# The product of V for the last 64 positions, before instead of behind the fourth product of V, in two of four batches

## The chip, the cores and the metric

The program runs on one core of a Trainium2 chip. Its time is the device time of one execution in microseconds (us). The engines are TensorE (PE; its weight loads are PEld), VectorE (DVE), ScalarE (ACT), GpSimd (POOL) and SyncE (SP), which issues the DMAs. Every engine has its own instruction queue, and engines wait for one another at semaphores.

## The reference

Three blocks follow one another, all in float32, over 4 batches of 576 positions and 512 features:

```
attention   8 heads of 64, window of 128 positions, a bias by distance; out = softmax(q k^T) v
gMLP        h = gelu(x @ w_in)              # 512 -> 1024
            u, v = h[:, :512], h[:, 512:]
            v_n = normalize(v) * g_ln       # mean and variance over the 512 features
            v_s = w_sg @ v_n + b_sg         # over the 576 positions
            x   = x + (u * v_s) @ w_out
GLU         h = relu(x @ w_in2); c = conv of 3 taps along the positions
            out = (h * sigmoid(c)) @ w_out2
```

The change concerns the products that make v in the gMLP of the first and of the last batch.

## The kernel before, in words

The kernel keeps about float32 accuracy with three matmuls where one would do in a single pass: each matrix is split into a high and a low part (tiles `hi`, `lo`), and hi*hi, hi*lo and lo*hi are added up in PSUM.

The work is cut into steps, and a written list gives their order. Letters name the kind of step, numbers the batch and the part. Lower-case steps prepare data, many of them weights: they clamp and rebuild numbers out of 64-bit words with five DVE instructions for each piece (lines 310 to 315, tile `wa`), and split them on ACT and POOL. The steps of the gMLP are:

- `V b.j` (function `m_v`): v for 128 positions (j = 0 to 3), 12 matmuls of 512 columns into a PSUM tile `psv`. j = 4 is the rest of 64 positions: four copies on POOL put the high and low parts of the last 64 positions side by side into tiles `xt`; then 8 matmuls run, and the two halves of the PSUM tile are added: ACT copies one half out (line 755), DVE adds the other (line 756, in the trace DVE L231 `v<-psv,v`). Only that addition frees the PSUM tile. With j < 4 one ACT instruction, the gelu, reads the tile and frees it.
- After that each V step goes through gelu, mean and variance (DVE L760, L761), the inverse root on POOL (L763, L764), the normalization (DVE L765) and the split into `vn` (ACT L222 the high part, DVE L231 the low part).
- `U b.half.m` (`m_u`): u, 12 matmuls into a PSUM tile `psu`, and a gelu on ACT.
- `G b.half.m` (`m_sg`): the product with w_sg, 14 matmuls into `pss`. It reads all five `vn` tiles of its batch, the one of j = 4 in the last two matmuls. DVE reads the result (L822).
- `W b.half.m` (`m_wo`): the product with w_out into `pso`.

`psv`, `psu`, `pss` and `pso` share one pool of two PSUM tiles (`gps`, bufs=2), so a product can start when the product two places before it in the list has been read out of PSUM. The steps C, E, N, T and A are the attention of a later batch (scores `sc` with their mask on DVE L435, exponentials on ACT L187, normalization, transposes, product with v). They run between the gMLP steps of the batch before.

The list gives priorities. A planner places the instructions of the steps into the queue of each engine, by costs of its own. A queue is worked off in order.

In batch 0, V2, U0.3 and V3 come before the scores of the next batch, V4 behind them, and U1.0, U1.1 next. In batches 1 and 2 V0 to V4 run in order, and scores stand behind V4. In batch 3, V0 to V4 are followed by eight U steps at once, since there is no attention left.

Of the kernel before, what the change touches and what calls it, by code (L numbers as in the profile page):

```python
# [54 lines left out]
def _steps():  # L55


    def of(p):
        return f"{p // NP}.{p % NP}"

    def scores(p):
        return [f"C{of(p)}"]

    def weigh(p):
        return [f"E{of(p)}", f"N{of(p)}"]

    def back(p):
        return [f"T{of(p)}", f"A{of(p)}"]

    def halves(p):  # L70
        return [f"X{of(p)}.0", f"X{of(p)}.1"]

    def loads(p):
        return [f"L{of(p)}", f"M{of(p)}"]

    weave = lambda main, more: [
        x for i, m in enumerate(main) for x in [m] + more[i * len(more) // len(main) : (i + 1) * len(more) // len(main)]
    ]
    put_by = [f"a{i}.{c}" for i in (1, 0) for c in range(16)]
    s = """  # L80
        l0.0 k0 l1.0 k5 l2.0 l3.0 v0.0 v1.0 v2.0 v3.0 j1.0 j1.1 l0.1
        c0.0 e0.0 c1.0 e1.0 n0.0 c2.0 e2.0 t0.0 n1.0 c3.0 e3.0 l1.1 j1.2 j1.3 v0.1 i1.0 z0.0 X0.0.0 t1.0 n2.0 z1.0 X0.1.0
        l2.1 v1.1 i1.1 t2.0 n3.0 z2.0 X0.2.0 c0.1 e0.1 l3.1 j0.0 i1.2 t3.0 z3.0 X0.3.0 c1.1 e1.1 v2.1 i1.3 n0.1 c2.1 e2.1 j0.1 v3.1 j0.2 t0.1 n1.1 z0.1
        i0.0 c3.1 e3.1 j0.3 k4 V0.0 t1.1 n2.1 z1.1 i0.1 V0.1 t2.1 n3.1 z2.1 i0.2 U0.0.0 i0.3 t3.1 z3.1 X0.0.1 U0.0.1
        X0.1.1 U0.0.2 X0.2.1 X0.3.1
    """.split()
    for b in range(B - 1):
        p = NP * (b + 1)
        V = [f"V{b}.{j}" for j in range(5)]
        U = [[f"U{b}.{half}.{m}" for m in range(4)] for half in range(2)]  # L90
        G = [[f"G{b}.{half}.{m}" for m in range(4)] for half in range(2)]
        W = [[f"W{b}.{half}.{m}" for m in range(4)] for half in range(2)]
        if b == 0:
            uv = ["g0", "g1", V[2], "g2", "o0.0", U[0][3], "g3", "o0.1", V[3]] + loads(p) + ["g4", "o1.0"] + scores(p) + ["o1.1", V[4], "o2.0", "o2.1"]
            uv += loads(p + 1) + U[1][:2] + ["o3.0"] + scores(p + 1) + ["o3.1"] + loads(p + 2) + U[1][2:] + scores(p + 2)
        else:
            uv = V[:2] + loads(p) + scores(p) + V[2:] + loads(p + 1) + scores(p + 1) + U[0] + loads(p + 2) + U[1][:1] + scores(p + 2) + U[1][1:]
        T, A = ([f"{x}{of(p + i)}" for i in range(4)] for x in "TA")
        gw = weigh(p) + G[0] + weigh(p + 1) + G[1][:1] + loads(p + 3) + T[:1] + G[1][1:2] + W[0][:1] + A[:1] + halves(p)
        gw += weigh(p + 2) + W[0][1:2] + T[1:2] + W[0][2:] + A[1:2] + scores(p + 3) + halves(p + 1) + weigh(p + 3) + T[2:3] + G[1][2:3]  # L100
        gw += A[2:3] + halves(p + 2) + G[1][3:] + T[3:] + W[1][:1] + A[3:] + halves(p + 3) + W[1][1:]
        if b == 0:
            s += uv + gw
        else:
            now = put_by[10 * b - 10 : 10 * b]
            s += weave(uv, now[:4]) + weave(gw, now[4:])
    first = " ".join(s)
    n = [f"V3.{j}" for j in range(5)] + [f"U3.{half}.{m}" for half in range(2) for m in range(4)]
    n += [f"G3.0.{m}" for m in range(4)] + ["G3.1.0"] + [f"W3.0.{m}" for m in range(4)]
    n += [f"G3.1.{m}" for m in range(1, 4)] + [f"W3.1.{m}" for m in range(4)]  # L110

    for m in range(4):
        n[n.index(f"U3.{m % 2}.{m // 2 + 1}")] += f" w0.{m // 2}.{m % 2}"
    n[n.index("W3.0.3")] += " y0.0"
    n[n.index("G3.1.2")] += " y0.1"
    n[n.index("W3.1.0")] += " y0.2"
    n[n.index("W3.1.1")] += " y0.3"
    s = weave(n[:-6], put_by[LATE:]) + n[-6:]
    late = [f"w1.{k}.{h}" for k in range(4) for h in range(2)]
    s = s[:-6] + weave(s[-6:], late)  # L120
    second = " ".join(["x0.0.1.2.3"] + s)
    return first, second


STEPS = _steps() + (
    """
    D0.0 D0.1 D0.2 D0.3 x1.0.1 D0.4 x1.2.3 D0.5 y1.0 D0.6 y1.1 D0.7 y1.2 y1.3 D1.0 D1.1 F0.0 D1.2 D1.3 F0.1 D1.4
# [964 lines left out]
```

## Time and profile before

| | |
|---|---|
| time, median of 3 runs | 563.36 us (562.4 to 564.08) |
| the profiled execution, time | 562.71 us |
| its span, first to last instruction | 560.6 us |
| mean granted TensorE clock | 0.988 |
| PE busy | 529.1 us (94%) |
| DVE busy | 375.0 us (67%) |

The times of the trace count from the start of the span. "Granted clock" is the share of TensorE's full speed that it was given: 1.00 is 2.4 GHz, 0.50 is 1.2 GHz. The name in brackets at the end of a timeline row is what ended the idle time of the engine before it.

### The profile page before, as it was taken

The numbers are of one execution on the slowest core, as the hardware profiler recorded it, in microseconds if no ns is written. First come the engines' busy times: TensorE is split into PE (matmuls) and PEld (weight loads), VectorE is DVE, ScalarE is ACT, GpSimd is POOL, SyncE is SP. The second block draws the span as 40 slices with busy tenths as digits, with TensorE's granted clock in tenths as the row PEclk, the third lists the DMA queues.
The fourth block names the chain that finished last, engine by engine and source line by source line (L and its number), as shares of the span: only waits on it lengthen the run. The fifth ranks groups of instructions, "written<-read, shape, count | busy, mean of one in ns | idle before, by whom it ended". The sixth has DMA issues, their size and how long they took to land.

```text
span 560.6 us, 11990 instructions
## 1 busy us (share of the span) xinstructions
PE 529.1 (94%) x4560; PEld 479.5 (86%) x4560; DVE 375.0 (67%) x961; ACT 252.1 (45%) x647; POOL 260.5 (46%) x407
## 2 busy tenths in 40 slices
PE   8988988999999999999998989996999999999997
PEld 7766777998898988998987979984998999999987
DVE  4968898764879766879777778668666434655300
ACT  6676549433358442376443212244545333444301
POOL 2435236741246362345534354388676354456500
PEclk9998988999999999999998999999999999999999
DMA  8973341332260765323553324710202210100111
GB/s 299 371 235 156 111 154 46 125 113 102 90 196 20 233 192 165 118 80 91 184 172 107 120 75 132 270 68 21 83 20 61 81 39 19 42 20 19 39 37 57
DMA packets 33209, 63.93 MB, mean 114 GB/s; under 512 B 3968, under 2 KB 13952, under 8 KB 33152
## 3 DMA queue, kind: packets, MB, share of 16 engines
q1 hardware_dynamic: 33008, 63.04, 33.8%
q8 instruction: 36, 0.59, 0.4%
q14 instruction: 21, 0.17, 0.1%
q10 hardware_dynamic: 144, 0.13, 0.1%
HBM read 48.47 MB, written 14.68 MB: 113 GB/s over the span
## 4 chain that ended last, share of the span: by engine, by line
PE 64%; DVE 13%; ACT 9%; POOL 6%; DMA 4%; issue 3%; SPq 1%; POOLq 0%; ACTq 0%; DVEq 0%
PE psg L213 31%; PE psu L213 7%; PE pso L213 7%; PE psv L213 5%; PE o L213 5%; ACT t L187 4%; PE pss L213 4%; PE sc L213 3%; PE pT L499 2%; POOL gl L231 2%; DVE t L242 1%; DMA w<-in_w_in_dram 1%; DMA x2d<-x 1%; DVE t L822 1%; POOL cc L242 1%
## 5 line engine op out<-in xcount | busy, mean ns | idle before, releaser
L213 PE MATMUL psg<-x2g,w 128*128 128x256 f32 (+1 forms) x768 | 105.8, 294 | 1.4 <-DVE x2g L231 0.9
L213 PEld LDWEIGHTS psg<-x2g,w 128*128 128x128 f32 x768 | 103.5, 188 | 3.4 <-DVE x2g L231 1.5
L213 PE MATMUL psg<-wout,gh 128*128 128x512 f32 (+1 forms) x272 | 80.4, 379 | 0.9 <-ACT gh L222 0.9
L187 ACT ACTIVATE t<-t,st 128x192 f32<-128x192 f32 (+1 forms) x144 | 61.9, 432 | 20.8 <-DVE st L435 20.8
L213 PE MATMUL pss<-wsg,vn 128*128 128x256 f32 (+1 forms) x448 | 65.0, 301 | 3.8 <-DVE t L822 3.6
L213 PEld LDWEIGHTS pss<-wsg,vn 128*128 128x128 f32 x448 | 61.4, 192 | 5.1 <-DVE t L822 5.1
L213 PE MATMUL psu<-xg,win 128*128 128x320 f32 (+1 forms) x384 | 58.1, 310 | 7.9 <-DVE v L231 4.6
L213 PEld LDWEIGHTS psu<-xg,win 128*128 128x128 f32 x384 | 54.7, 199 | 9.9 <-DVE v L231 5.1
L950 DVE SCALAR_TENSOR_TENSOR cc<-hb,cw,cc 128x576 f32<-128x576 f32 x32 | 27.6, 865 | 48.3 <-POOL cc L242 48.3
L213 PEld LDWEIGHTS psg<-wout,gh 128*128 128x128 f32 x272 | 49.5, 188 | 10.2 <-ACT gh L222 1.7
L213 PE MATMUL psg<-wout,gl 128*128 128x512 f32 (+1 forms) x136 | 51.7, 380 | 3.7 <-POOL gl L231 3.7
L213 PE MATMUL pso<-gh,wo 128*128 128x256 f32 (+1 forms) x256 | 53.0, 301 | 1.8 <-DVE t L822 1.8
L213 PE MATMUL psv<-win,xg 128*128 128x512 f32 x192 | 47.8, 398 | 1.9 <-ACT win L222 0.9
L242 POOL TENSOR_SCALAR cc<-hb,cw 128x576 f32<-128x576 f32 x32 | 28.9, 904 | 43.4 <-ACT hb L946 43.4
L231 POOL TENSOR_TENSOR gl<-gg,gh 128x512 fp32r<-128x512 f32 x32 | 46.0, 1437 | 0.6
L435 DVE CUSTOM_DVE_ANT_0 t<-sc,tab 128x192 f32<-128x192 f32 (+1 forms) x144 | 40.4, 334 | 6.1 <-PE sc L213 6.1
L213 PEld LDWEIGHTS psv<-win,xg 128*128 128x128 f32 x192 | 35.3, 188 | 10.0 <-POOL win L231 1.9
L213 PEld LDWEIGHTS pso<-gh,wo 128*128 128x128 f32 x256 | 40.4, 188 | 3.8 <-DVE t L822 2.8
L231 DVE TENSOR_TENSOR gg<-cc,hb 128x576 f32<-128x576 f32 x32 | 31.3, 983 | 16.9 <-ACT cc L187 16.9
L946 ACT ACTIVATE hb<-psg 128x576 f32<-128x576 f32 x32 | 20.6, 651 | 47.2 <-PE psg L213 47.2
L231 POOL TENSOR_TENSOR t<-t,u 128x256 f32<-128x256 f32 (+1 forms) x32 | 26.7, 837 | 29.4 <-DVE t L822 29.2
L213 PE MATMUL pso<-gl,wo 128*128 128x256 f32 (+1 forms) x128 | 37.1, 297 | 1.3 <-DVE gl L231 1.3
(97 smaller groups left out, 965.9 us busy)
## 6 DMA issues: line engine op xcount, KB each, us to landing
V<-in_v_dram SPq DMA_DIRECT2D x12, 704.0 KB, 4.9
x2s<-x2d SPq DMA_DIRECT2D x16, 288.0 KB, 3.1
w<-in_w_in_dram SPq DMA_DIRECT2D x8, 512.0 KB, 6.6
w<-in_w_out_dram SPq DMA_DIRECT2D x16, 256.0 KB, 2.8
w<-in_w_in_dram SPq DMA_DIRECT2D x16, 256.0 KB, 2.7
wout<-w2d SPq DMA_DIRECT2D x8, 512.0 KB, 6.9
q<-in_q_dram SPq DMA_DIRECT2D x12, 320.0 KB, 3.6
out_dram<-ot SPq DMA_DIRECT2D x15, 256.0 KB, 2.0
```

The costliest lines, as they stand in the source:

```text
L187: ins = nc.scalar.activation(*args, **kw)
L213: return nc.tensor.matmul(out, lhsT, rhs, start=start, stop=stop, **kw)
L231: return (nc.vector if eng == "dve" else nc.gpsimd).tensor_tensor(dst, a, b, op=op)
L242: e.tensor_scalar(dst, src, col, 1.0, op0=ALU.mult, op1=ALU.mult)
L435: nc.vector.tensor_tensor_reduce(e, bank, table, scale=-SCALE, scalar=3e38, op0=ALU.add, op1=ALU.min, accum_out=mx)
L499: grouped(nc.tensor.transpose(ps[:, i * P : (i + 1) * P], src, ident), first and i == 0, waits if i == 0 else ())
L822: nc.vector.scalar_tensor_tensor(t1, o, gln[:, d : d + 1], bsg[:, sl], op0=ALU.mult, op1=ALU.add)
L946: nc.scalar.activation(h[:, 1 : S + 1], ps[:, 256 : 256 + S], AF.Relu)
L950: nc.vector.scalar_tensor_tensor(cc, h[:, 0:S], cw[:, 0, c : c + 1], cc, op0=ALU.mult, op1=ALU.add)
```

## The change

In the lists of batch 0 and batch 3 the steps V3 and V4 change places. In batch 0 everything that stood between them keeps its place: the loads and scores of the next batch's first pair of heads, a piece of w_sg (g4) and two pieces of w_out (o1.0, o1.1) now stand behind V4 and ahead of V3. In batch 3 the two are neighbours. Batches 1 and 2 are as they were.

```diff
-            uv = ["g0", "g1", V[2], "g2", "o0.0", U[0][3], "g3", "o0.1", V[3]] + loads(p) + ["g4", "o1.0"] + scores(p) + ["o1.1", V[4], "o2.0", "o2.1"]
+            uv = ["g0", "g1", V[2], "g2", "o0.0", U[0][3], "g3", "o0.1", V[4]] + loads(p) + ["g4", "o1.0"] + scores(p) + ["o1.1", V[3], "o2.0", "o2.1"]
...
-    n = [f"V3.{j}" for j in range(5)] + [f"U3.{half}.{m}" for half in range(2) for m in range(4)]
+    n = [f"V3.{j}" for j in (0, 1, 2, 4, 3)] + [f"U3.{half}.{m}" for half in range(2) for m in range(4)]
```

## Rows read from the trace of the kernel before

**Rows 1.** The page: busy us (share of the span) and instructions, two engines' line.
```profile
PE 529.1 (94%) x4560; PEld 479.5 (86%) x4560; DVE 375.0 (67%) x961; ACT 252.1 (45%) x647; POOL 260.5 (46%) x407
```
**Rows 2.** Waits of PE: total us, how often, the longest.
```profile
PE psu L213 <- DVE v L231: 4.6, 2, 2.5
...
PE pss L213 <- DVE t L822: 3.6, 3, 2.3
```
**Rows 3.** Timeline of PE, batch 0: start us, us, what, count [idle <-releaser].
```profile
61.55 2.90 PE L213 MATMUL psv<-win,xg 128*128 128x512 f32 x12
...
66.06 2.15 PE L213 MATMUL psv<-win,xt 128*128 128x512 f32 x8
68.05 1.92 PE L213 MATMUL psu<-xg,win 128*128 128x320 f32 x12
72.50 2.94 PE L213 MATMUL psu<-xg,win 128*128 128x320 f32 x12 [2.53 <-DVE v L231]
```
**Rows 4.** Timeline of PE, batch 3.
```profile
289.10 11.12 PE L213 MATMUL psv<-win,xg 128*128 128x512 f32 x48
300.05 1.99 PE L213 MATMUL psv<-win,xt 128*128 128x512 f32 x8
301.88 1.55 PE L213 MATMUL psu<-xg,win 128*128 128x256 f32 x12
305.51 12.93 PE L213 MATMUL psu<-xg,win 128*128 128x256 f32 x84 [2.08 <-DVE v L231]
...
322.74 3.56 PE L213 MATMUL pss<-wsg,vn 128*128 128x256 f32 x28 [1.00 <-DVE t L822]
```
**Rows 5.** Windows of 1 us behind two waits (PE, PEld, DVE, ACT, POOL, clock, DMA).
```profile
91.00:92.00 1.00, 0.98 (x5) 0.69 (x4) 1.00 (x3) 1.00 (x6) 1.00 (x3) 0.50 0.00 0
306.00:307.00 1.00, 1.00 (x7) 1.00 (x7) 0.96 (x3) 0.98 (x3) 0.79 (x1) 0.50 0.91 281
```
**Rows 6.** Timeline of DVE: V4's addition in batch 1.
```profile
147.85 0.68 DVE L231 TENSOR_TENSOR v<-psv,v 64x512 f32<-64x512 f32 x1
```
**Rows 7.** Timeline of PE, batch 1, around its V4.
```profile
144.71 1.99 PE L213 MATMUL psv<-win,xt 128*128 128x512 f32 x8
```
**Rows 8.** Timeline of POOL: the last copy into xt, batches 0 and 3.
```profile
57.56 0.67 POOL L225 TENSOR_SCALAR xt<-xg 128x128 fp32r<-128x128 f32 x1 [1.50 <-DVE xg L231]
294.12 0.30 POOL L225 TENSOR_SCALAR xt<-xg 128x128 fp32r<-128x128 f32 x1 [3.17 <-DMA x2d<-x]
```
**Rows 9.** The chain that ended last, batch 0: start us, us, what.
```profile
81.87 0.41 ACT wo L222
82.27 0.34 ACT u L187
...
88.48 0.48 DVE t L822
```
**Rows 10.** One window of batch 0: columns as in rows 5.
```profile
62.60:84.30 21.70, 19.17 (x213) 17.03 (x212) 20.19 (x79) 9.65 (x19) 6.03 (x10) 0.92 0.50 164
```
**Rows 11.** Timeline of DVE: its one longer wait in that window.
```profile
76.81 0.29 DVE L435 CUSTOM_DVE_ANT_0 t<-sc,tab 128x128 f32<-128x128 f32 x1 [0.56 <-PE sc L213]
```
**Rows 12.** The chain that ended last, batch 3.
```profile
310.47 0.51 ACT vn L222
...
311.72 0.42 DVE wa L315
312.17 2.53 DMA w<-in_w_in_dram
...
322.21 0.49 DVE t L822
```
**Rows 13.** Timeline of DVE: V4's last instruction in batch 3.
```profile
311.00 0.68 DVE L231 TENSOR_TENSOR vn<-v,vn 64x512 fp32r<-64x512 f32 x1 [1.34 <-ACT vn L222]
```
**Rows 14.** The chain that ended last, later.
```profile
358.04 0.66 ACT hb L946
...
394.98 162.63 PE psg L213 x963
```

## The prediction

> **What bounds the kernel now.** I read the page first: PE is busy for 94% of the span and DVE for 67% [rows 1]. The kernel as a whole follows PE, so what is worth asking is where PE waits. The view of waits answers it: the longest entry is U's product waiting for DVE's addition of V4's two halves, 4.6 us in two waits [rows 2]. The timelines of PE show where: in batch 0 at 72.50, after 2.53 us [rows 3], and in batch 3 at 305.51, after 2.08 us [rows 4]. Both are U's second product. It takes the PSUM tile that V4 had, and V4's tile is free only after ACT's copy and DVE's addition. Windows of 1 us then show a second price: within two microseconds of PE's return from a wait of 2 us, the granted clock is 0.50 (1.2 GHz); a window behind each of two waits is shown, of two to three such windows each time [rows 5].
>
> The chain that ended last shows what comes next: shortly after both places PE waits again, for DVE's L822, which frees the PSUM tile of the first G product [rows 2, 4, 9]. Time that PE gains at U reaches the end only if that L822 comes earlier too.
>
> **What the change removes, adds and moves.** No instruction is added or removed. V3 and V4 keep their 12 and 8 matmuls, V4 its four POOL copies, one ACT copy and one DVE addition, and both the chain to `vn`. Neither step issues a DMA. In the list V4 is moved ahead of the loads of the next batch (on SP), a piece of w_sg, two pieces of w_out and the scores, V3 behind them; in batch 3 only V3 and V4 trade places. SP's own order is the same but for what the planner makes of it.
>
> *The cover of V4's read-out.* In batch 0 V4 ends at 66.06 + 2.15 = 68.21 and the waiting U starts at 72.50, 4.3 us later; only U1.0 (1.92 us) stands between [rows 3]. In the new order V4 starts at 61.55, where V3 did. Behind it run the scores and V3, and the first of the U products takes V4's tile. Scores and V3 fill 66.06 - 61.55 = 4.5 us, more than the 4.3. I take the wait as gone: 2.5 us. In batch 3 V4 ends at 302.04 and U goes on at 305.51, 3.5 us later, behind 1.55 us of U [rows 4]. Afterwards V3 is the cover, a quarter of 300.05 - 289.10, or 2.7 us. The read-out need not take 3.5 us: in batch 1, where scores stand behind V4, it ended at 147.85 + 0.68 = 148.53 [rows 6], 1.8 us after V4's end at 144.71 + 1.99 = 146.70 [rows 7]. So 0 to 0.8 us of the wait stays, and 1.3 to 2.1 us goes.
>
> *The clock.* The second U in batch 0 took 2.94 us instead of the first's 1.92 us [rows 3]. That is 1.0 us on one product; the low clock goes on over part of what follows, so I estimate 1.5 us of lost work each time from this row and the number of low windows [rows 5]. So PE is free about 4 us earlier in batch 0 and 3 to 3.5 us earlier in batch 3.
>
> *What could be late for V4.* Its POOL copies must be done sooner. The last one ends at 57.56 + 0.67 = 58.23 in batch 0 and at 294.42 in batch 3 [rows 8]; V4 would start at 61.55, and in batch 3 at V3's old start, 289.10 + 3 x 2.74 = 297.3. The margins are 3.3 and 2.9 us. I cost this at nothing; the cover is V3's old predecessors, V2 and U0.3, on PE. In batch 3 the copy waits for the DMA that writes x2d [rows 8]; one 3 us later would be paid in full. V3 is now the last to become `vn`, but G needs its high part only in its tenth matmul, and V3's read-out is one instruction shorter than V4's.
>
> *What comes through, batch 0.* L822 at 88.48 stands in DVE's queue behind a normalization that needs the exponentials, and ACT starts these after the last gelu of U at 82.27, which stands behind a cast of a w_out piece at 81.87 that waits for DVE [rows 9]. DVE is the engine to look at: from 62.60 to 84.30 it was busy for 20.19 of 21.70 us [rows 10]. What it must do is unchanged. Of its 1.5 us of idle time the one longer wait, 0.56 us for scores that came behind the late U [rows 11], goes away. The gain has the bounds 0 (DVE's order unfavourable) and 1.5 us (all idle time gone), unless ACT's queue puts the gelu ahead of the cast. I take 0.6 us, the wait that PE's lateness explains.
>
> The Trainium skill, PSUM — Partial Sum Buffer, section Engine vs sequencer instructions, says that the queues of ScalarE, VectorE and GpSimd are strictly first in, first out. Here the trace agrees: the addition of V4 and L822 start late behind other work of DVE. By that rule alone an earlier product is read no earlier than its place in the queue, and with an unchanged place the sum of this batch would be zero.
>
> *What comes through, batch 3.* L822 at 322.21 stands behind weight pieces that wait for DMAs, and these DMAs wait for buffers that DVE's L315 at 311.72 frees [rows 12]. L315 stands behind V4's low part at 311.00, before which DVE idled 1.34 us for ACT's cast [rows 13], and that cast stood in ACT's queue behind a gelu of U, so behind PE [rows 12]. With PE 3 us earlier this wait is gone: 1.3 us. The bounds are 0 (the last cast of V3 stands behind a gelu as well) and 2.1 us (the whole wait of PE).
>
> *To the end.* From 89 us to the V products of batch 3 the chain is mostly PE; later it passes at 358.04 from PE to ACT, to POOL and DVE, and from 394.98 on it is PE again to the end [rows 14]. All that starts earlier when PE does. So 0.6 + 1.3 = 1.9 us: 562.71 - 1.9 = 560.8 us against the profiled execution. That one is 0.65 us below the median of the three runs, 563.36, so on their scale the forecast is 561.5 us, 0.34% faster (1.9 of 563.36). A change of under 0.3% (1.7 us) is about what a measurement of this kernel cannot tell from none.
>
> **Rivals.**
> 1. *All of it is given back at G.* DVE's order keeps L822 where it is, and PE waits there instead: 563.4 us, at most 0.6 less. For it speak the nearly full DVE [rows 10] and the DMAs ahead of L822 [rows 12]; against it the two idle times of DVE that PE causes [rows 11, 13].
> 2. *More comes through.* The planner, seeing V4's addition earlier, puts the last gelu and the exponentials ahead of weight pieces, and L822 with them. At most 2.53 + 2.08 us of waits and 2 x 1.5 us of clock, 7.6 us, so 555.8; half of it gives 559.6 us. Against it: the w_out pieces stand earlier in the list than U.
> 3. *Slower: the clock falls at G instead of at U.* PE arrives at G 3 to 4 us earlier, and if L822 moves by only 1 us, the wait before it grows from 2.3 us [rows 2] to 5 in batch 0, and from 1.0 [rows 4] to about 3 in batch 3. Waits of 2 us were followed by half clock, the one of 1.0 us was not [rows 4, 5]. In batch 3 the fall would then hit G and W, which the end waits for, and cost 1.5 us; in batch 0 a second stretch at half clock would cost another 1.5 us. It decides once the gains are under these costs: with nothing gained at L822, 563.4 + 1.5 to 3.0, about 565 us. Against it: in batch 0 a clock that falls during the wait itself costs nothing there.
>
> The Trainium skill, TensorE: Matmul & The Clock Gate, section A second HAM failure mode: psum-queue depth-cycling, tells of a kernel that loses throughput because PE idles briefly between groups as it cycles through PSUM tiles, and pays for slowing down and coming back. Rows 5 agree; that is rival 3.
>
> **Chances, range.** The forecast 0.45 (two thirds of it beyond 0.3%, the rest within), rival 1 0.27 (one ninth of it slower), rival 2 0.13, rival 3 0.15 (a fifth of it within 0.3%). That makes faster 0.43, same 0.42, slower 0.15. The forecast's own range is 559.8 (both upper bounds, 1.5 + 2.1 us) to 563.4 (both lower ones). To leave out no more than 2 in 10 I extend to 558.8, which takes in half of rival 2, and to 564.2, which takes in rival 1 and the mild end of rival 3.
>
> **What would show it.** Right: no wait of U for the addition of V4, or less than 0.8 us in batch 3; no half clock there; exponentials of batch 0 some 0.6 us earlier; L315 and L822 of batch 3 some 1.3 us earlier; the wait of PE at G longer. Wrong: L822 where it was (rival 1), clock at 0.50 in the G and W products of batch 3 (rival 3), V4 waiting for a copy on POOL, or queues that the planner has reordered well beyond the two steps.

## The result, and the profile after

The changed kernel takes **557.76 us** (median of 6 runs, 556.95 to 559.3), the kernel before 563.47 us on the same chip (6 runs, 561.99 to 564.08). The ratio is 0.9906, 95% interval 0.9882 to 0.993: 5.7 us faster, where 1.9 us were forecast. The time lies below the range. The profiled execution is the longest of the six, 559.3 us, with a span of 557.2 us.

The page and PE's waits (total us, how often, the longest) answer to [rows 1, 2]:

```profile
PE 527.5 (95%) x4560; PEld 477.2 (86%) x4560; DVE 373.1 (67%) x961; ACT 252.1 (45%) x647; POOL 263.0 (47%) x407
...
PE pss L213 <- DVE t L822: 4.2, 3, 1.7
PE psg L213 <- POOL gl L231: 2.8, 3, 1.1
PE sc L213 <- DVE st L435: 2.1, 1, 2.1
...
PE psu L213 <- DVE v L231: 0.3, 1, 0.3
```

U's wait for V4's addition went from 4.6 to 0.3 us. In its place stand a new wait of the scores for DVE's masks (2.1 us) and 0.6 us more for L822. These three alone would leave 4.3 - 2.1 - 0.6 = 1.6 us.

PE's timeline of batch 0 after the change answers to [rows 3], that of batch 3 to [rows 4]:

```profile
61.45 2.01 PE L213 MATMUL psv<-win,xt 128*128 128x512 f32 x8
...
65.07 3.06 PE L213 MATMUL psv<-win,xg 128*128 128x512 f32 x12
67.97 3.68 PE L213 MATMUL psu<-xg,win 128*128 128x320 f32 x24
...
80.33 1.42 PE L213 MATMUL sc<-k,q 64*64 64x192 f32 x24 [2.09 <-DVE st L435]
81.45 3.60 PE L213 MATMUL pss<-wsg,vn 128*128 128x256 f32 x28
86.59 6.01 PE L213 MATMUL pss<-wsg,vn 128*128 128x256 f32 x42 [1.55 <-DVE t L822]
...
288.50 8.41 PE L213 MATMUL psv<-win,xg 128*128 128x512 f32 x36
296.75 1.99 PE L213 MATMUL psv<-win,xt 128*128 128x512 f32 x8
298.58 2.90 PE L213 MATMUL psv<-win,xg 128*128 128x512 f32 x12
301.73 1.63 PE L213 MATMUL psu<-xg,win 128*128 128x256 f32 x12 [0.26 <-DVE v L231]
303.67 11.39 PE L213 MATMUL psu<-xg,win 128*128 128x256 f32 x84 [0.30 <-ACT v L187]
...
320.09 3.80 PE L213 MATMUL pss<-wsg,vn 128*128 128x256 f32 x28 [1.73 <-DVE t L822]
```

In batch 0 both U products now run in one piece (24 matmuls in 3.68 us; before, 1.92 us, a wait of 2.53 and 2.94 us). In batch 3 84 matmuls of U take 11.39 us, not 12.93. Windows of 1 us (PE, PEld, DVE, ACT, POOL, clock, DMA) behind the start of the second G of batch 0 (now at 86.59) and of U in batch 3 (now at 301.73), about as far as those of [rows 5], show full clock where those had 0.50:

```profile
89.00:90.00 1.00, 1.00 (x11) 1.00 (x10) 0.96 (x3) 1.00 (x6) 1.00 (x4) 1.00 0.00 0
302.00:303.00 1.00, 1.00 (x11) 1.00 (x11) 1.00 (x3) 0.97 (x2) 0.00 (x0) 1.00 0.00 0
```

**Where the time came from.** I take the start of the same PE product in both traces; the difference is how far the changed kernel leads. Before U's waiting product in batch 0 the lead is zero. It is 2.78 us at that product (72.50 before), 4.41 us at the next U product, only 2.42 us at the second G (89.01 before, 86.59 after), and 2.19 us at the end of batch 0. In between, the second G runs at full clock (its 42 matmuls take 6.01 us, not 7.37) and the lead is 3.76 us at the transposes behind it (96.21 before, 92.45 after); up to the end of the batch this is given back, where PE now waits 1.1 us for L822 and for POOL's low part `gl`. The lead falls to 0.60 us at V3.0 (289.10 before, 288.50 after): the code and the queues of batches 1 and 2 are the same, and a DMA, shown below, landed later. Batch 3 brings it back to 2.19 us, and the first batch of the last stage, whose code is untouched, adds 1.24 us: 3.43 us at the end.

**Batch 0: the planner moved the cast.** ACT's timeline after the change:

```profile
77.14 0.41 ACT L222 CAST wo<-wa 128x256 fp32r<-128x256 f32 x1 [0.20 <-DVE wa L315]
77.45 0.76 ACT L187 ACTIVATE u<-psu 128x320 f32<-128x320 f32 x2
78.23 1.28 ACT L187 ACT_TABLE_LOAD   x1
79.52 0.40 ACT L187 ACTIVATE t<-t,st 128x128 f32<-128x128 f32 x1
...
82.94 0.39 ACT L222 CAST wo<-wa 128x256 fp32r<-128x256 f32 x1
```

And the same place before the change:

```profile
81.87 0.41 ACT L222 CAST wo<-wa 128x256 fp32r<-128x256 f32 x1 [1.67 <-DVE wa L315]
82.18 0.44 ACT L187 ACTIVATE u<-psu 128x320 f32<-128x320 f32 x1
82.63 1.28 ACT L187 ACT_TABLE_LOAD   x1
83.93 0.40 ACT L187 ACTIVATE t<-t,st 128x128 f32<-128x128 f32 x1
```

Before, the fourth cast of a w_out piece (o1.1) stood ahead of the last gelu of U and waited for DVE. After, it stands among the exponentials, at 82.94, and the two last gelus run back to back from 77.45. The exponentials begin 4.4 us earlier. L822 comes 2.4 us earlier, as DVE's timeline shows, after the change:

```profile
82.29 0.42 DVE L315 SCALAR_TENSOR_TENSOR wa<-wst,wa 128x256 uint32<-128x256 uint32 x1
...
86.11 0.42 DVE L822 SCALAR_TENSOR_TENSOR t<-pss,gln,bsg 128x256 f32<-128x256 f32 x1
86.45 0.37 DVE L310 TENSOR_SCALAR wa<-wst 128x256 uint32<-128x256 uint32 x1
```

and before:

```profile
83.75 0.29 DVE L310 TENSOR_SCALAR wa<-wst 128x256 uint32<-128x256 uint32 x1
...
87.04 0.42 DVE L315 SCALAR_TENSOR_TENSOR wa<-wst,wa 128x256 uint32<-128x256 uint32 x1
...
88.22 0.35 DVE L482 TENSOR_SCALAR r<-st 128x9 f32<-128x9 f32 x1 [0.48 <-ACT t L187]
88.48 0.47 DVE L822 SCALAR_TENSOR_TENSOR t<-pss,gln,bsg 128x256 f32<-128x256 f32 x1
```

DVE finishes o1.1 no sooner than before (82.29 against 81.41, 0.9 us later); it is only that the exponentials do not wait for it now. And a further piece, five instructions from 83.75 to 87.04, or 1.7 us of DVE, stood ahead of L822 before and begins at 86.45 now, behind L822. What each of these two moves is worth alone was not separated.

**The last stage.** The planner also gave POOL another order there, although no step of it was touched. POOL's timeline before:

```profile
385.84 0.32 POOL L231 TENSOR_TENSOR gr<-gg,gr 128x64 fp32r<-128x64 f32 x1
386.12 1.77 POOL L231 TENSOR_TENSOR gl<-gg,gh 128x512 fp32r<-128x512 f32 x1
```

and in a second profile of the changed kernel (e3 below):

```profile
380.99 1.80 POOL L231 TENSOR_TENSOR gl<-gg,gh 128x512 fp32r<-128x512 f32 x1
382.75 0.83 POOL L231 TENSOR_TENSOR gr<-gg,gr 128x64 fp32r<-128x64 f32 x1
```

The low part `gl`, for which PE waits, now comes ahead of the edge's low part. PE's wait for it went from 3.7 us (the row before: 3, longest 1.6) to 2.8 us. ACT's and PE's own order of the stage are new as well.

### The profile page after: what moved, and what is told of

The parts are those of the page before. It is cut to its first block, busy times and chain, and to the rows that moved or that the text cites. A ratio compares the mean times of both kernels' runs of the same rounds, so it can differ in the third digit from the quotient of the medians.

```text
span 557.2 us, 11992 instructions
## 1 busy us (share of the span) xinstructions
PE 527.5 (95%) x4560; PEld 477.2 (86%) x4560; DVE 373.1 (67%) x961; ACT 252.1 (45%) x647; POOL 263.0 (47%) x407
## 4 chain that ended last, share of the span: by engine, by line
PE 59%; DVE 15%; POOL 11%; ACT 7%; DMA 5%; issue 3%; SPq 0%; POOLq 0%; ACTq 0%; DVEq 0%
PE psg L213 31%; PE pso L213 7%; PE psu L213 5%; PE o L213 4%; ACT t L187 4%; PE pss L213 3%; PE sc L213 3%; PE psv L213 3%; POOL t L242 2%; POOL gl L231 2%; DVE t L435 2%; PE pT L499 2%; DMA x2d<-x 2%; DVE t L242 1%; POOL cc L242 1%
## 5 line engine op out<-in xcount | busy, mean ns | idle before, releaser
L213 PE MATMUL pss<-wsg,vn 128*128 128x256 f32 (+1 forms) x448 | 63.8, 297 | 4.5 <-DVE t L822 4.2
L213 PEld LDWEIGHTS pss<-wsg,vn 128*128 128x128 f32 x448 | 60.1, 188 | 6.0 <-DVE t L822 5.9
L213 PE MATMUL psu<-xg,win 128*128 128x320 f32 (+1 forms) x384 | 55.8, 302 | 3.5 <-POOL win L231 1.6
L213 PEld LDWEIGHTS psu<-xg,win 128*128 128x128 f32 x384 | 52.5, 192 | 5.5 <-POOL win L231 2.0
```

The lines of the kernel that those rows point to most:

```text
L213: return nc.tensor.matmul(out, lhsT, rhs, start=start, stop=stop, **kw)
```

## The experiments

Four theories were in play: **A**, the gain of batch 0 comes through by the cast's new place; **B**, it comes through by PE's earlier arrival alone; **C**, the last stage's new order is a gain of its own; **D**, the gain is chance, of the kind that differs between runs of one kernel. Each kernel runs beside the kernel before on the same chip; its median there was 562.62 (e1 to e4), 563.42 (e5 to e8) and 562.31 us (e10 to e13).

**One batch at a time (e1, e2), and the change again (e3).** e1 keeps only the first hunk of the diff, e2 only the second, e3 is the changed kernel.

```diff
# e1: batch 0 alone
-"o0.1", V[3]] + loads(p) + ["g4", "o1.0"] + scores(p) + ["o1.1", V[4],
+"o0.1", V[4]] + loads(p) + ["g4", "o1.0"] + scores(p) + ["o1.1", V[3],
# e2: batch 3 alone
-for j in range(5)] + [f"U3.
+for j in (0, 1, 2, 4, 3)] + [f"U3.
```

> Only batch 0 has V4 ahead of V3; batch 3 is as before. Theory 1 (the planner's orders): PE leads by about 2.2 us when batch 1 begins, and the last stage, whose POOL queue order also changes with this edit alone, adds about 1.2 us: 3.4 us, about 560.0 us against 563.4. In the trace the fourth cast of a w_out piece stands behind the last gelu of U, and exponentials begin near 79.5 us instead of 83.9. Theory 2 (only the wait of PE counts, as predicted): 0.6 us, about 562.8 us. The wait of 2.1 us of batch 3 stays in both.

> Only batch 3 has V4 ahead of V3; batch 0 is as before. Theory 1: 1.5 us through L822 of batch 3, and 1.2 us from the last stage, whose POOL order also changes with this edit alone: 2.7 us, about 560.7 us. Theory 2 (the wait of PE and nothing in the last stage): 1.3 to 1.5 us, about 562.0 us, with the waits on POOL between 355 and 395 us as before.

> The changed kernel once more, unaltered, for a second profile and a narrower interval. Theory: its first profile, 559.3 us, is the longest of six runs because a DMA of x2d took 5.1 us in batch 2 and held up a POOL copy, which cost 1.7 us of a lead of 2.2; a second profile should be near 557.5 us and keep a lead of about 1.8 to 2.2 us over the kernel before through batch 2. Rival: the loss in batch 2 comes each time with the changed order; then the second profile loses about 1.5 us there as well.

Measured: e1 558.78 us, ratio 0.9928 (0.9902 to 0.9953); e2 560.84 us, 0.9963 (0.994 to 0.9987); e3 556.86 us, 0.989 (0.9866 to 0.9914). Each half gains, and batch 0 gains several times the 0.6 us forecast. e3's profile repeats batch 0 to 0.02 us (lead 2.17), but it does not lose in batch 2 as the first profile did (lead 2.25 at V3.0), and leads by 6.16 us at the end. So the fall of the lead in batch 2 does not come each time; but e1, e4 and e5 lost 1.3 to 1.9 us in batches 1 and 2 as well (table below), so that it is chance alone is not shown. Both e1 and e2 have the new order in the last stage.

**The cast tied to its old place (e4).** The changed kernel, but U's last gelu of batch 0 must follow the cast of o1.1.

```diff
-        act(u, ps[:, :n], AF.Gelu_apprx_tanh)
+        gelu = act(u, ps[:, :n], AF.Gelu_apprx_tanh)
+        if (b, half, m) == (0, 1, 3):
+            tc.add_manual_dep(gelu.ins, cast[1, 1].ins.name, follow, reason="pin")
```

> The changed kernel with the cast of the fourth w_out piece (o1.1) held ahead of the last gelu of U in batch 0, on ACT, as in the kernel before; otherwise unaltered. Theory 1 (the gain in batch 0 comes from the planner placing this cast behind the gelu): exponentials begin 1 us or more later than 79.5 us and 1.0 to 1.6 us of the gain goes, about 559 us. Rival (the wait of PE alone made the gain, the cast's place doesn't matter): the time of the changed kernel within 0.4 us, about 557.8 us.

Measured: 562.28 us, ratio 0.9981 (0.9961 to 1.0002). PE's wait for V4 and the half clock stay away (lead 4.39 us behind U's second product), and yet the lead at the end of batch 0 is -0.76 us where the changed kernel had 2.19. ACT's timeline of e4:

```profile
77.50 0.43 ACT L187 ACTIVATE u<-psu 128x320 f32<-128x320 f32 x1
82.79 0.41 ACT L223 CAST wo<-wa 128x256 fp32r<-128x256 f32 x1 [4.85 <-DVE wa L316]
83.10 0.44 ACT L187 ACTIVATE u<-psu 128x320 f32<-128x320 f32 x1
83.56 1.28 ACT L187 ACT_TABLE_LOAD   x1
84.85 0.40 ACT L187 ACTIVATE t<-t,st 128x128 f32<-128x128 f32 x1
```

ACT idles 4.85 us for the piece and the exponentials start at 84.85, 0.9 us later than before the change. But with the tie the planner also placed instructions of DVE, ACT, POOL and PE between 84 and 108 us anew. Among them L822 (L829 in e4) now stands ahead of the normalization, 1.6 us earlier than before the change:

```profile
86.90 0.48 DVE L829 SCALAR_TENSOR_TENSOR t<-pss,gln,bsg 128x256 f32<-128x256 f32 x1
```

So PE still leads by 1.23 us at the second G (1.10 us in e12 below), and loses that and more between there and the end of the batch. B falls: the earlier arrival alone did not come through. A is supported, but how much of the 2.9 us is the cast's, and how much is what the planner placed anew behind it, is not separated. That e4 lost 5.4 us against e3, and not only the 2.9 us of batch 0, was open; e12 takes it up.

**The last stage tied to its old order (e5).** The changed kernel, with the taps, splits and sigmoids of the last stage's first batch tied on POOL and ACT to the order that they had before.

```diff
+    def pin(b, ins, at):
+        if b == 0 and at:
+            tc.add_manual_dep(ins.ins, kin[at[1]][at[0]].ins.name, follow, reason="pin")
...
+        pin(b, hb, {5: ("sig", 3), 6: ("sig", 4)}.get(c))
+        pin(b, tap, {4: ("lo", 2), 5: ("hi", 3), 7: ("hi", 5)}.get(c))
+        pin(b, sig, {4: ("gh", 2)}.get(c))
```

> The changed kernel, with the POOL and ACT queues of the last stage's first batch (GLU, 355 to 395 us) pinned to the order that they have in the kernel before; V4 stays ahead of V3. Theory: 1.0 to 1.5 us of the gain arises there, from the planner's new POOL order, so the time is 558.3 to 559 us where the changed kernel has about 557.3. Rival: the order doesn't matter there, POOL being full either way; the same time within 0.4 us.

Measured: 559.28 us, ratio 0.993 (0.9902 to 0.9958). The last stage adds 0.28 us to the lead instead of 1.24 and 1.46. But the tie put back the old order only in part. PE's own order in the stage is still new, and on POOL so is the very pair shown above:

```profile
383.79 1.29 POOL L232 TENSOR_TENSOR gl<-gg,gh 128x512 fp32r<-128x512 f32 x1
385.04 0.83 POOL L232 TENSOR_TENSOR gr<-gg,gr 128x64 fp32r<-128x64 f32 x1
```

And the loss does not support C: PE's waits between 366 and 410 us add up to 4.5 us in e5 as in e3, against 5.5 us in the kernel before, so the tie brought none of them back. The clock fell in e5 (0.50 from 390 to 392 us) and not in e3; e11 below, with the new order untied and 0.50 in the same window, adds 0.21 us.

**The copies into xt in a buffer of their own (e6, e7).** The trace shows one thing that differs between runs of one kernel: V4's last copies on POOL wait for the DMA `x2d<-x`, since their buffer is shared, and everything behind them on POOL waits too. The changed kernel's row in the view of waits, and its worst case on POOL's timeline:

```profile
POOL xt L225 <- DMA x2d<-x: 15.4, 6, 5.0
```

```profile
213.78 0.30 POOL L225 TENSOR_SCALAR xt<-xg 128x128 fp32r<-128x128 f32 x1 [4.96 <-DMA x2d<-x]
...
215.80 0.19 POOL L763 TENSOR_SCALAR rs<-ba 128x1 f32<-128x1 f32 x1
```

The inverse root of V0's normalization stands behind this copy. The same wait was 3.50 us in batch 2 of the kernel before. e6 (the changed kernel) and e7 (the kernel before) take a buffer of another group from batch 1 on. DVE's and ACT's queues stay as they were, POOL's does not: in batches 1 and 2 the planner placed three of the four copies earlier, in e6 as in e7, which the expectations below did not foresee. In batch 3 the order is unchanged.

```diff
-            xt = [mpool.tile([P, 320], F32R, tag="t1", name="xt", bufs=NT1)[:, :P] for _ in range(NK)]
+            if b:
+                own = mpool.tile([P, S], F32R, tag="u", name="xt", bufs=4)
+                xt = [own[:, k * P : (k + 1) * P] for k in range(NK)]
+            else:
+                xt = [mpool.tile([P, 320], F32R, tag="t1", name="xt", bufs=NT1)[:, :P] for _ in range(NK)]
```

> The changed kernel, with the four xt pieces of batches 1 to 3 in a tile of their own instead of tiles that the write of x2 to memory still holds; all queue orders stay the same, only POOL's wait for the x2d DMA is gone. Theory: that wait costs 1 to 1.7 us in batch 2 and 0 to 1.5 us in batch 3 by chance of the DMA, so the time falls by 1.5 to 2.5 us to about 555.5 us and spreads less from run to run. Rival: the wait is covered; 557.3 us and the same spread.

> The kernel before with the same tile of its own for xt in batches 1 to 3, queue orders as in the kernel before. Theory: 1.5 to 3 us less than 562.6, about 560.5 us, with the second U of batch 3 waiting less than 2.1 us for V4's addition, and the distance to the changed kernel with the same tile is what the exchange of V3 and V4 is worth without the DMA's chance: 3.5 to 5 us. Rival: no difference to the kernel before.

Measured: e6 **555.34 us**, ratio 0.9876 (0.9855 to 0.9897), four runs within 1.8 us; e7 560.69 us, 0.9965 (0.9949 to 0.998). The change is worth 5.35 us without this DMA's wait (560.69 - 555.34), so D does not explain the gain. e6 is the fastest kernel here and beats the kernel before; against the changed kernel its interval overlaps (0.9882 to 0.993), so its lead over that one is likely, not shown.

PE's timeline in batch 3, first e7 (old order), then e6 (new order):

```profile
303.05 11.40 PE L213 MATMUL psu<-xg,win 128*128 128x256 f32 x84 [0.33 <-DVE v L231]
...
319.70 3.56 PE L213 MATMUL pss<-wsg,vn 128*128 128x256 f32 x28 [1.96 <-DVE t L826]
```

```profile
299.58 12.85 PE L213 MATMUL psu<-xg,win 128*128 128x256 f32 x96
...
316.55 3.79 PE L213 MATMUL pss<-wsg,vn 128*128 128x256 f32 x28 [0.81 <-DVE t L826]
```

With the buffer of its own the old order waits only 0.33 us for V4's addition, so most of the 2.08 us of [rows 4] was the DMA's; it waits 1.96 us at G instead, the new order 0.81.

**The piece moved by hand in the kernel before (e8).** If the cast of o1.1 is what holds the exponentials, moving the step o1.1 behind the next scores should help without the change.

```diff
-scores(p) + ["o1.1", V[4], "o2.0", "o2.1"]
+scores(p) + [V[4], "o2.0", "o2.1"]
...
-scores(p + 1) + ["o3.1"]
+scores(p + 1) + ["o1.1", "o3.1"]
```

> The kernel before, V3 and V4 in the old order, with the w_out piece o1.1 written behind the scores and so behind U in the list of batch 0. Theory (the exponentials need both, PE's U early and the cast out of its way): PE ends the last U at 81.5 us as before, so the exponentials can begin at most 0.7 us earlier: 562.0 to 562.6 us. Rival (the cast alone held the exponentials): 2 us or more gained, about 560.5 us.

Measured: 560.03 us, ratio 0.9951 (0.993 to 0.9971). The time is better, but not for the reason tested: the exponentials begin at 83.12 and the second G some 0.8 us earlier, yet the lead at the end of batch 0 is -1.0 us. The gain arises in the last stage (2.6 us), whose queues the planner had changed as well. This run does not support A, since what G gained was lost behind it, and it is a second case of an untouched stage that pays.

**The halves and the ties again, without the DMA (e10 to e13).** e1, e2, e4 and e5, each with the edit of e6.

> Only batch 0 has the new order, and xt of batches 1 to 3 has a buffer of its own, so that no copy of POOL waits for the write of x2d. The two kernels with that buffer stand at 560.7 us (old order) and 555.3 us (new order in both batches). Theory: the exchange in batch 0 passes 2.2 us on by the cast that the planner placed behind the exponentials, and some 1.2 us more arise in the last stage by its new POOL order: 560.7 - 3.4 = 557.3 us. Rival (batch 0 is worth only the 0.6 us of the prediction, and what the single runs showed was the DMA's chance): 560.1 us, or 558.9 with the last stage's 1.2 us.

> Only batch 3 has the new order, xt of batches 1 to 3 with a buffer of its own. In the kernel of before with that buffer, U in batch 3 waited only 0.3 us for V4's addition, so little is left to gain there. Theory: batch 3 gives 0.3 to 1.0 us and the last stage's new order some 1.2 us: 560.7 - 1.9 = 558.8 us. Rival (batch 3's exchange is worth the whole 2 to 3 us that it seemed to give with the shared buffers): 560.7 - 3 - 1.2 = 556.5 us. Rival (the last stage gives nothing by itself): 560 us.

> The changed kernel with xt in a buffer of its own (555.3 us), and the last gelu of U in batch 0 tied behind the fourth cast of a w_out piece, as in before. Theory (the gain of batch 0 comes through by the place of that cast): 2.2 us or, by the earlier pinned run's loss at batch 1, 2.9 us are gone: 557.5 to 558.2 us. Rival (PE's vanished wait and clock pass the gain on by themselves): 555.3 us. If it is 560 us, as the earlier pinned run had it without this buffer, the tie costs something in later batches as well, and not the DMA's chance.

> The changed kernel with xt in a buffer of its own (555.3 us), and in the first batch of the last stage POOL and ACT tied to the order that they had before the change. Theory (the planner's new order in the last stage is worth 1.2 to 1.5 us): 556.5 to 556.8 us. Rival (that gain was only a shift of waits, given back by the end, or a chance of the clock): 555.3 us. If it is 557.5 us or more, the old order costs more behind an earlier start than it did in the kernel of before.

Measured: e10 557.34 us, ratio 0.9913 (0.9888 to 0.9938); e11 557.59 us, 0.9927 (0.99 to 0.9954); e12 557.86 us, 0.9922 (0.9901 to 0.9943); e13 557.3 us, 0.9897 (0.9873 to 0.9921). e10 came where A and C put it. e12 is 2.5 us above e6, within the 2.2 to 2.9 us that A gave, and their intervals don't overlap; the planner placed 84 to 108 us anew here too, as in e4. The further loss of e4 did not come again without the DMA's wait. e11 lies between theory and rival. e13's median is 2.0 us above e6's, more than C's 1.2 to 1.5, but they ran beside different runs of the kernel before: by ratios the distance is 1.2 us and the intervals overlap. Falls of the clock are in it: e13's runs go from 555.23 us at a mean granted clock of 0.994 to 559.38 us at 0.982, while e6's have 0.991 or 0.994. So e13 does not show C either.

What each stage added to the lead over the kernel before, from single profiles (us; start of the same PE products at 113.39, 289.10, 375.11 and 554.55 in the trace before):

| kernel | batch 0 | batches 1, 2 | batch 3 | last stage | half clock in the last stage |
|---|---|---|---|---|---|
| changed | 2.19 | -1.59 | 1.59 | 1.24 | yes |
| e3 changed | 2.17 | 0.08 | 2.45 | 1.46 | no |
| e1 batch 0 | 2.04 | -1.85 | 1.84 | 1.00 | yes |
| e2 batch 3 | -0.03 | -0.53 | 3.31 | -0.65 | yes |
| e4 cast tied | -0.76 | -1.32 | 1.04 | 1.24 | no |
| e5 last stage tied | 2.01 | -1.38 | 1.31 | 0.28 | yes |
| e6 changed, own xt | 1.81 | 0.51 | 3.40 | 1.41 | no |
| e7 before, own xt | -0.03 | 0.74 | 2.39 | -2.06 | yes |
| e10 batch 0, own xt | 2.18 | 0.03 | 2.23 | 1.32 | no |
| e11 batch 3, own xt | -1.40 | 0.45 | 3.42 | 0.21 | yes |
| e12 cast tied, own xt | -1.13 | 1.42 | 3.43 | 1.20 | no |
| e13 last stage tied, own xt | 0.81 | 0.34 | 3.31 | -1.11 | yes |

Batch 0: 1.8 to 2.2 us in all six with the new order and no tie there (e13's 0.81 had lost 1.3 us by 55 us, ahead of the change; e11's -1.40 likewise began 0.7 us late). Batch 3: with a shared buffer it scatters; with its own, 3.3 to 3.4 us in the new order against 2.2 to 2.4 in the old, so 0.9 to 1.2 us. Last stage: without half clock 1.2 to 1.5 us in the new order, in five profiles, against 0 in the kernel before, which had none either; with half clock in the same windows (386 to 394 us), -0.65 in the new order (e2) against -2.06 in the old (e7), again 1.4 us apart. So the stage's new plan as a whole pays, and C holds in that sense. The tied kernels lie at -1.11 (e13, the windows of e2) and 0.28 (e5, the window of e11, which has 0.21), within 0.5 us of the new order: what the ties put back pays little, if anything. Whether it is the pair on POOL or PE's own order that pays was not separated. Put together, 2.2 + 1.1 + 1.3 = 4.6 us of the 5.35. The remaining 0.8 us stays open; falls of the clock may be in it, and each ratio is uncertain by about 0.0025, or 1.4 us.

## Why the prediction was wrong

**Right: the cover.** V4's wait in batch 0 is gone; in batch 3 0.26 us stay (forecast 0 to 0.8). POOL's copies were in time, with the margin worked out: the last ends at 293.85 in batch 3, V4 starts at 296.75.

**Right: the clock.** From the first to the last of the low windows PE's lead rose by 1.63 us in batch 0 (2.78 to 4.41) and by 1.53 us in batch 3 (1.85 to 3.38); the estimate was 1.5 us each. PE was free 4.4 us earlier in batch 0 (forecast about 4) and 3.38 - 0.60 = 2.8 us in batch 3 (3 to 3.5). The first window of [rows 5] stands behind the second G, not behind U; that third fall, 7.37 against 6.01 us, was not priced, and what it gave was lost again by the end of the batch.

**The step that failed: "What comes through, batch 0", 0.6 us.** 2.2 us came through, above its upper bound of 1.5. The price was read from DVE's idle time with the orders of DVE and ACT taken as given. The sentence held the exception, "unless ACT's queue puts the gelu ahead of the cast", and that is what happened; on DVE, another piece also went behind L822. Rival 2 named this and got 0.13, on the argument that the w_out pieces stand earlier in the list than U. The list's order is only a priority: the new queue has the cast of o1.1 behind U's gelus though the list has o1.1 ahead of them. In e4 and e12, with the cast tied, PE is 4.4 us early at U and the batch ends 0.8 to 1.1 us later than before. So the gain of this batch needs the planner's new order; that the cast's place alone decides it is not shown, since the tie changed other queues behind it.

The Trainium skill, PSUM — Partial Sum Buffer, section Engine vs sequencer instructions, has the queues of ScalarE, VectorE and GpSimd strictly first in, first out. The traces agree: ACT idled 4.85 us at the tied cast with a gelu behind it. What the prediction made of that, "with an unchanged place the sum of this batch would be zero", came true in sum in e4 and e12, where the cast's place was unchanged, but not by L822: it came 1.6 us earlier in e4, and the gain was lost behind it.

**About right: "What comes through, batch 3", 1.3 us** (0 to 2.1). L315 came at 310.20 instead of 311.72 and L822 at 319.56 instead of 322.21, from a start 0.60 us earlier. The 1.59 us of this stage in the one profile prove little, since e1, with the old order there, gained 1.84 us. Without the DMA the exchange is worth 0.9 to 1.2 us, so the size was about right. The wait that was to be removed was misread, though: most of it was the DMA's. In e7, with the old order, 1.75 of the 2.08 us are gone.

**Missing: a term for stages whose code is untouched.** "All that starts earlier when PE does" was taken to move as one block. The planner ordered the last stage anew and that brought 1.2 to 1.5 us (e3, e4, e6, e10 and e12 against the kernel before, all without half clock there). The ties of e5 and e13 did not take it away. Why an exchange in batch 0 alone, or in batch 3 alone, changes the plan of the last stage was not tried; that the plan's times there shift is only argued.

**The other rivals.** Rival 1 (all given back at G) did not come: in batch 0 the lead of 4.41 us fell to 2.42 at G and not to zero, and e4 and e12, which gave all back, did so behind the second G. Rival 3 (half clock at G): in the changed kernel's first profile the clock was 1.00 through G and W of batch 3 (316 to 336 us) and around G in batch 0. In e3 it was 0.50 from 81 to 83 us, in the first G of batch 0, behind the new wait of the scores; that cost 1 us there (lead 0.67 instead of 1.63 us at the first G) and nothing at the end of the batch (2.17 and 2.19 us): PE then did not wait for L822 at the second G, where the first profile has 1.55 us. In batch 3 it happened in e10, with the old order there: behind its wait of 2.15 us for L822 the clock was 0.50 from 320 to 322 us.

## What to carry to other kernels

Where a planner places the instructions, a price that rests on "this queue's order stays" needs its own check: ask which instruction heads the queue of the engine that passes the gain on, and what it is worth if the planner moves it. Here holding one cast of 0.4 us, with all that the planner placed anew behind it, cost 2.9 us. Look at the untouched stages of the trace after, too, since they are planned anew, and compare the queues of an experiment with those it is read against: here one tie and one buffer made the planner move other instructions too, and another tie missed a pair. And before comparing two profiles stage by stage, take a second profile, because one transfer that blocks a queue moved a stage by up to 1.9 us, and a fall of the clock one by 2.1 us.

## What was not expected of the hardware

**The DMA x2d.** From issue to the copy behind it, the same write took 3.13 and 4.30 us in batches 2 and 3 of the kernel before, 4.48 and 4.32 in the changed kernel, 3.44 and 3.91 in its second profile, but 1.93 or 1.94 us in batch 1 each time. POOL stands still for it, with what other engines need behind it. Why it varies was not tried.

**A fall of the clock that comes and goes.** In the last stage, between 386 and 394 us, the clock fell to 0.50 in some profiles and not in others of the same kernel: the changed kernel fell, e3 did not. One window each of the changed kernel and of e7:

```profile
386.00:391.00 5.00, 4.17 (x16) 3.54 (x17) 3.28 (x3) 2.95 (x6) 3.46 (x7) 0.66 0.17 42
```

```profile
384.00:392.00 8.00, 5.93 (x22) 4.98 (x23) 6.21 (x6) 3.54 (x6) 4.97 (x7) 0.69 0.16 50
```

Seven of the twelve profiles in the table have it. Among the kernels with the new order in that stage, the four of nine that fell added 0.45 us on average there (1.24, 1.00, -0.65, 0.21), the five that did not 1.33 us; the two tied kernels and e7 fell, and the kernel before did not. Whether the new order makes the fall rarer can't be told from so few.

**One wait, with and without a fall.** The scores' wait of 2.09 us in batch 0, for DVE's masks, was followed by full clock in each window from 80 to 86 us in the changed kernel's first profile, and by 0.50 in its second (e3):

```profile
81.00:82.00 1.00, 1.00 (x19) 0.88 (x12) 1.00 (x6) 1.00 (x5) 0.00 (x0) 0.50 0.20 71
```

Of the nine profiles with the new order in batch 0, six fell there (e1, e3, e4, e6, e12, e13) and three did not (the first, e5, e10), behind the same wait of 2.08 to 2.10 us. The waits of 2.08 to 2.53 us before the change were followed by 0.50.
